# GQA attention, forward and backward, on one core: K, V, dK and dV laid out with 8 KB per partition, q and grad_out packed, every DMA on the sync queue

## The chip, the core and the metric

The kernel runs on one core of a Trainium2 chip, with nothing on the other cores. Its engines are TensorE (PE, with its weight loads shown as PEld), VectorE (DVE), ScalarE (ACT), GpSimd (POOL) and SyncE (SP); they run side by side and meet through semaphores. Data moves between DRAM and the on-chip memory by 16 DMA engines, which are fed by queues: SP's queue is called q1 in the profile, POOL's queue q0, and q8 and q14 fetch instructions. The metric is the device time of one execution in microseconds, the median over several runs.

## The reference

For 32 batches, 32 query heads with 4 query rows each share 4 key/value heads of 2,048 rows and width 128. The kernel must return the attention output and the gradients of q, k and v for a given grad_out. All tensors are bf16.

```python
B, Hq, Hkv, Sq, Sk, D = 32, 32, 4, 4, 2048, 128
k = jnp.repeat(k, rep, axis=1)
v = jnp.repeat(v, rep, axis=1)
scores = jnp.einsum("bhqd,bhkd->bhqk", q, k) * D ** -0.5
p = softmax(scores, axis=-1)
out = jnp.einsum("bhqk,bhkd->bhqd", p, v)
dq, dk, dv = vjp(grad_out)
```

K and V are read once (2 MiB each for one batch), dK and dV are written once (2 MiB each), and q, grad_out, out and dq are 32 KiB each for one batch. So a batch moves 8 MiB of large tensors and 128 KiB of small ones.

## The kernel before

One batch is cut into named units (function `units_of`, from line 172 on): loads `LQ` (q and grad_out), `LK` and `LV` (each in two pairs of heads g=0,1, 1 MiB a pair); transposes of K and V on PE (`KT`, `VT`, L372) with their copies out of PSUM (`KTe`, `VTe`, L337 on ACT or L340 on DVE); scores, maximum, exponential and row sum (`S` L383, `MX` L390, `EX` L399, `L` L402 and L404); GpSimd's scaled copies of grad_out and q (`dop` L411, `qp` L419, `rs` L423); the output (`O` L442, `Oe` L449 or L451) and its store `Os`; the gradient path (`DL` L456, `DP` L383, `DS` L463); `DV` and `DK` (L477) with their copies `DVe`, `DKe` (L483) and stores `DVs`, `DKs` (L492); and `DQ` (L442), `DQe` and the store `DQs`. ET and DT (L431) are the transposes of e and ds. For the last batch alone the stores of dV and dK go out in halves (`DVh`, `DKh`, L488).

The order is written out by hand. `plan` gives each unit a planned time, b * PERIOD plus the value of `PLACE`, plus a shift for the first three and the last four batches (`SHIFT`); all units of all batches are sorted by that time, and each engine runs its own units in that order. An engine that waits holds up all that is behind it on the same engine. That goes for SP too: a store that waits for its data holds up the loads that are planned after it. `DMA, SMALL = "SP", "POOL"` sends the large transfers to SP's queue and the small ones (`LQ`, `Os`, `DQs`) to POOL's, where they stand in line with `dop`, `qp` and `rs`.

On SP, every DMA takes the next of eight semaphores in turn, and in the built program each DMA from the ninth on waits for the DMA eight before it: no more than eight of SP's DMAs are under way at a time.

K has 8 tile buffers of 1 MiB, V has 4, and the outgoing dV and dK share 6 (`CAP`). In DRAM each head of K is 2,048 rows of 256 bytes, one after the other. A partition holds 16 rows, that is 4,096 contiguous bytes, for each of the pair's two heads; the heads are 512 KiB apart. A 1 MiB transfer is therefore 256 pieces of 4,096 bytes. q and grad_out are loaded as 128 rows of 256 bytes each, into tiles of their own for each batch, and out and dq are stored likewise.

Of the kernel before, what the change touches and what calls it, by code (L numbers as in the profile page):

```python
# [10 lines left out]
BF16 = mybir.dt.bfloat16  # L11
ACT = mybir.ActivationFunctionType
ALU = mybir.AluOpType
AX = mybir.AxisListType

P = 128
NH = 4
# [3 lines left out]
DMA, SMALL = "SP", "POOL"  # L21
# [4 lines left out]
    LQ=[-47.936], LK=[-16.977, -14.467], LV=[3.599, 0.95], QT=[-7.484], QTe=[-6.947], KT=[2.869, 1.617, 7.32, 1.994,  # L26
    -5.235, 5.431, 1.272, 6.997], KTe=[4.732, 3.093, 7.43, 5.007, -4.213, 5.728, 1.38, 7.728], VT=[10.378, 12.043,
    11.732, 10.779, 22.772, 19.387, 22.024, 28.632], VTe=[11.121, 12.155, 12.993, 11.722, 23.303, 21.604, 22.619,
    29.88], S=[7.995, 8.089, 10.109, 10.191], MX=[9.431, 10.828], EX=[11.829, 13.307], L=[13.33], dop=[14.332],
    qp=[18.579], rs=[18.682], ET=[13.658, 17.08], ETe=[14.252, 17.097], DT=[33.736, 36.072], DTe=[35.413, 37.066],  # L30
    O=[17.693, 18.002, 18.156, 18.29], Oe=[18.672], Os=[94.455], DQ=[49.509, 49.546, 51.434, 51.658], DQe=[52.911],
    DQs=[136.569], DL=[19.54], qfree=[23.411], ofree=[103.245], rfree=[77.997], DP=[19.952, 20.297, 32.139, 32.573],
# [14 lines left out]
        qp=[-26.573], rs=[12.305], ET=[-63.892, -40.448], ETe=[-47.865, -38.526], DT=[-4.086, -0.412], DTe=[-3.298,  # L47
        6.139], O=[-39.845, -33.444, -32.183, -28.165], Oe=[-27.877], Os=[-59.712], DQ=[1.765, 2.888, 1.329, 1.269],
        DQe=[1.892], DQs=[-81.021], DL=[-24.403], qfree=[-3.591], ofree=[-33.901], rfree=[9.398], DP=[-14.103,
# [6 lines left out]
        LQ=[-243.022], LK=[-211.953, -145.031], LV=[-16.995, -65.672], QT=[-143.905], QTe=[-60.636], KT=[-16.483,  # L56
        -14.108, -10.124, 0.716, -51.009, -13.779, -3.931, -2.747], KTe=[-17.567, -13.982, -6.982, -0.41, -31.758,
        -9.805, 5.197, -0.622], VT=[-0.807, 8.201, 5.214, 2.135, 10.997, 1.446, 6.104, 4.85], VTe=[0.517, 9.075,
        5.788, 2.568, 12.326, 2.03, 6.271, 3.992], S=[-0.29, 0.211, -1.108, -0.674], MX=[-1.051, -0.497], EX=[2.148,
        0.721], L=[7.117], dop=[8.675], qp=[10.349], rs=[25.4], ET=[1.855, 2.426], ETe=[1.513, 3.358], DT=[13.036,  # L60
        7.483], DTe=[12.538, 6.893], O=[3.459, 3.832, 3.884, 5.102], Oe=[4.915], Os=[-60.332], DQ=[0.889, 1.045,
        -0.411, 0.94], DQe=[0.233], DQs=[-25.356], DL=[5.409], qfree=[12.194], ofree=[-66.5], rfree=[13.969],
        DP=[6.763, 7.072, 3.675, 3.981], DS=[7.015, 3.749], DV=[6.331, 5.5, 3.952, 3.37], DVe=[5.694, 4.344, 4.713,
        4.559, 2.372, 4.222, 1.681, 2.935], DVs=[2.104, -0.302], DVh=[148.344, 585.76, 528.125, 504.253], DK=[1.08,
        3.543, 0.508, 3.091], DKe=[3.833, 4.036, 2.313, 3.472, 1.048, -0.802, 2.792, 1.943], DKs=[9.575, 1.2],
# [8 lines left out]
        O=[1.246, 1.5, 1.545, 1.726], Oe=[1.403], Os=[-52.917], DQ=[1.425, 1.546, 0.484, 0.395], DQe=[-0.47],  # L74
        DQs=[-55.959], DL=[0.669], qfree=[3.492], ofree=[-33.606], rfree=[5.069], DP=[1.794, 1.829, 0.034, -0.258],
# [10 lines left out]
        O=[-1.322, -1.479, 0.528, 1.287], Oe=[1.058], Os=[87.413], DQ=[8.174, 8.908, 7.1, 7.978], DQe=[8.064],  # L86
        DQs=[153.09], DL=[1.413], qfree=[433.476], ofree=[379.582], rfree=[188.9], DP=[2.141, 2.215, 0.855, 0.51],
# [10 lines left out]
        DTe=[13.249, 14.741], O=[4.22, 3.956, 3.979, 4.659], Oe=[5.161], Os=[124.411], DQ=[53.76, 58.627, 71.647,  # L98
        76.742], DQe=[81.838], DQs=[178.343], DL=[4.74], qfree=[223.784], ofree=[169.959], rfree=[350.347],
# [11 lines left out]
        123.716], O=[14.871, 15.992, 19.77, 20.459], Oe=[24.605], Os=[65.93], DQ=[226.498, 229.962, 296.861,  # L111
        321.979], DQe=[324.799], DQs=[716.368], DL=[24.893], qfree=[188.487], ofree=[315.264], rfree=[471.673],
# [12 lines left out]
        Oe=[158.875], Os=[319.648], DQ=[364.485, 371.073, 501.046, 588.268], DQe=[601.801], DQs=[743.423],  # L125
        DL=[177.07], qfree=[296.09], ofree=[481.606], rfree=[573.081], DP=[203.332, 207.071, 280.92, 280.696],
# [36 lines left out]
    "0131321056372566642742270600202020220020440", "5454547463637160146371372260420466424246204"]  # L163
class Unit:
# [87 lines left out]
def plan(n_batches):  # L252
    tail = {n_batches + b: b for b in SHIFT if b < 0}
    order, bank_of = [], {}
    for b in range(n_batches):
        seen, banks = collections.Counter(), iter(BANK[b])
        special = tail.get(b, b)
        for u in units_of(b):
            name = u.key[1]
            i = seen[name]  # L260
            seen[name] += 1
            u.at = b * PERIOD + PLACE[name][i] + (SHIFT[special][name][i] if special in SHIFT else 0.0)
            if len(u.eng) == 2:
                u.on = ENGINE[name][i]
                if special in SWAP and SWAP[special].get(name, "-" * 16)[i] == "x":
                    u.on = "D" if u.on == "A" else "A"
                u.on = "ACT" if u.on == "A" else "DVE"
            else:
                u.on = next(iter(u.eng), "")
            if name in (NOT_LAST if b == n_batches - 1 else ONLY_LAST):  # L270
                u.on = ""
            for r in u.opens:
                if r[1] == "ps":
                    bank_of[r] = int(next(banks))
            order.append(u)
    return sorted(order, key=lambda u: u.at), bank_of

@with_exitstack
def kernel(
    ctx: ExitStack,  # L280
    tc: tile.TileContext,
    q: bass.AP,
    k: bass.AP,
    v: bass.AP,
    grad_out: bass.AP,
# [5 lines left out]
    nc = tc.nc  # L291
    B, Hq, Sq, D = q.shape
    Hkv, Sk = k.shape[1], k.shape[2]
    assert D == P and Hq * Sq == P and Hkv == NH and Hq // Hkv * Sq == 32
# [20 lines left out]
    rows = lambda t: t.rearrange("b h s d -> b (h s) d")  # L315
    pairs = lambda t: t.rearrange("b (g h) (p c) d -> b g p h (c d)", c=C, h=2)
    q_r, go_r, o_r, dq_r = rows(q), rows(grad_out), rows(out_0), rows(out_1)
    k_r, v_r, dk_r, dv_r = pairs(k), pairs(v), pairs(out_2), pairs(out_3)
# [23 lines left out]
    def emit(u):  # L342
        b, name, arg = u.key[0], u.key[1], u.key[2:]
        t = T[b]
        if name == "LQ":
            t["q"] = sm_pool.tile([P, D], BF16, name="q_sb")
            nc.gpsimd.dma_start(out=t["q"][:], in_=q_r[b])
            t["go"] = sm_pool.tile([P, D], BF16, name="go_sb")
            nc.gpsimd.dma_start(out=t["go"][:], in_=go_r[b])
        elif name in ("LK", "LV"):  # L350
            g, = arg
            p_, src = (k_pool, k_r) if name == "LK" else (v_pool, v_r)
            x = p_.tile([P, 2, C, D], BF16, name="k_sb" if name == "LK" else "v_sb")
            for h in range(2):
                t[name[1], 2 * g + h] = x[:, h]
            whole = x[:].rearrange("p h c d -> p h (c d)")
            for h in range(2) if b == 0 else [slice(0, 2)]:
                nc.sync.dma_start(out=whole[:, h], in_=src[b, g][:, h])
        elif name == "QT":
            ps = t["qtp"] = bank(b, "qt", dt=BF16)  # L360
            nc.tensor.transpose(out=ps[:, 0, :], in_=t["q"][:], identity=ident[:])
            nc.tensor.transpose(out=ps[:, 1, :], in_=t["go"][:], identity=ident[:])
# [81 lines left out]
        elif name in ("Oe", "DQe"):  # L444
            x, by = ("o", "rinv") if name == "Oe" else ("dq", "rs")
            t[x] = sm_pool.tile([P, D], BF16, name=x + "_sb")
            src = t[name[:-1]][:, 0:D]
            if u.on == "ACT":
                nc.scalar.activation(out=t[x][:], in_=src, func=ACT.Copy, scale=t[by][:])  # L449
            else:  # L450
                nc.vector.tensor_scalar(out=t[x][:], in0=src, scalar1=t[by][:], scalar2=None, op0=ALU.mult)  # L451
        elif name in ("Os", "DQs"):
            nc.gpsimd.dma_start(out=(o_r if name == "Os" else dq_r)[b], in_=t["o" if name == "Os" else "dq"][:])
        elif name == "DL":
            t["dl"] = sm_pool.tile([P, 1], FP32, name="delta")
            nc.vector.tensor_tensor_reduce(out=junk[:], in0=t["o"][:], in1=t["go"][:], scale=1.0, scalar=0.0,  # L456
# [43 lines left out]
_INS = ['q', 'k', 'v', 'grad_out']  # L500
_OUTS = [((32, 32, 4, 128), 'bfloat16'), ((32, 32, 4, 128), 'bfloat16'), ((32, 4, 2048, 128), 'bfloat16'), ((32, 4, 2048, 128), 'bfloat16')]
# [24 lines left out]
```

## Time and profile before

| | value |
|---|---|
| median of 6 runs | 692.4 us (691.51 to 698.01) |
| the profiled execution | 698.01 us, its span 696.2 us, 1.8 us lie around the span |
| PE busy | 622.3 us, 89% |
| ACT busy | 603.5 us, 87% |
| DVE busy | 558.5 us, 80% |
| POOL busy | 207.9 us, 30% |
| DMA | 274.47 MB in 75,005 packets, mean 394 GB/s |
| read / written in DRAM | 136.31 MB / 136.31 MB |
| POOL's DMAs | 128 of 32 KB: 5.7 us (loads) and 5.9 to 6.0 us (stores) from issue to landing |
| TensorE clock granted | 0.995 of full speed |

The profiled execution is the longest of the six, 5.6 us above the median. A packet is one piece of a transfer as a DMA engine handles it; each DMA also ends in a packet of 4 bytes on each of its 16 engines that counts the semaphore up. The share of a queue is the time that its packets took, as a share of the time of all 16 engines. The shares of the four queues add up to a little over 100%, because the time in which packets of two queues are under way on one engine counts for both. DMA is near saturation in 38 of the page's 40 slices, at 380 to 417 GB/s; the first slice has 346 GB/s, the last two 257 and 262.

### The profile page before, as it was taken

Reading aid. Unit: us, or ns where it says so; the run is one execution under the profiler, and the core shown is the slowest. Engines: PE = TensorE matmul, PEld = TensorE weight load, DVE = VectorE, ACT = ScalarE, POOL = GpSimd, SP = SyncE. Lnnn points to the kernel's source line nnn. Section 1 sums busy time; section 2 is a strip of 40 time slices with the busy share of each in tenths; the row PEclk is TensorE's granted clock in tenths of the full one; section 3 lists DMA queues with packets and bytes.
Section 4 is the critical chain, followed back from the end, with each engine's and each line's share of the span. In section 5 each row is a group of like instructions: output and inputs, shape, how many; then the busy total and the mean of one; then the engine's idle time right before and its main releaser. Section 6 shows DMA issues by size and latency. Waiting matters only on the chain.

```text
span 696.2 us, 28403 instructions
## 1 busy us (share of the span) xinstructions
PE 622.3 (89%) x12352; PEld 468.6 (67%) x12352; DVE 558.5 (80%) x776; ACT 603.5 (87%) x921; POOL 207.9 (30%) x426
## 2 busy tenths in 40 slices
PE   5899999999999999989999898998898988989984
PEld 4676677777667777666767666676666766766663
DVE  2788888888888888878888878787787877878785
ACT  2889999999999999988889888899888988988883
POOL 2423321333332233331233321333312333113330
PEclk9999999999999999999999999999999999999999
DMA  8999999999999999999999999999999999999967
GB/s 346 395 393 381 417 413 412 416 415 415 416 415 410 413 399 404 397 411 411 405 408 409 406 397 408 388 393 400 402 404 398 397 387 383 408 401 389 387 257 262
DMA packets 75005, 274.47 MB, mean 394 GB/s; under 512 B 6272, under 2 KB 6272, under 8 KB 74880
## 3 DMA queue, kind: packets, MB, share of 16 engines
q1 hardware_dynamic: 70784, 268.45, 97.4%
q0 software_dynamic: 4096, 4.20, 1.8%
q8 instruction: 96, 1.57, 0.8%
q14 instruction: 29, 0.24, 0.1%
HBM read 136.31 MB, written 136.31 MB: 392 GB/s over the span
## 4 chain that ended last, share of the span: by engine, by line
DMA 53%; PE 24%; ACT 11%; issue 5%; POOL 3%; DVE 3%; SPq 0%; POOLq 0%; DVEq 0%; ACTq 0%
DMA v_sb<-in_v_dram 52%; PE psum L372 11%; PE psum L477 6%; ACT dk_sb L483 4%; ACT dv_sb L483 3%; PE psum L431 3%; PE psum L442 2%; POOL dop_sb L411 2%; ACT e_sb L399 2%; ACT vt_sb L337 1%; PE psum L383 1%; DVE kt_sb L390 1%; DMA go_sb<-in_grad_out_dram 1%; DMA out_dram<-dv_sb 1%; DVE vt_sb L340 1%
## 5 line engine op out<-in xcount | busy, mean ns | idle before, releaser
L411 POOL TENSOR_SCALAR dop_sb<-go_sb,rinv 32x128 bf16<-32x128 bf16 x128 | 76.8, 600 | 446.3 <-DVE rinv L404 272.3
L483 ACT CAST dk_sb<-psum 128x1024 bf16<-128x1024 f32 x159 | 157.6, 1013 | 26.9 <-PE psum L477 21.0
L372 PE MATMUL psum<-ident,v_sb 128*128 128x128 bf16 x2048 | 148.3, 220 | 22.1 <-DMA v_sb<-in_v_dram 20.4
L483 ACT CAST dv_sb<-psum 128x1024 bf16<-128x1024 f32 x155 | 151.7, 1023 | 13.2 <-PE psum L477 12.4
L372 PEld LDWEIGHTS <-v_sb 128*128 128x128 bf16 x2048 | 118.5, 98 | 62.8 <-issue 31.9
L372 PE MATMUL psum<-ident,k_sb 128*128 128x128 bf16 x2048 | 142.8, 221 | 10.3 <-ACT dk_sb L483 10.2
L372 PEld LDWEIGHTS <-k_sb 128*128 128x128 bf16 x2048 | 121.8, 99 | 27.2 <-issue 24.4
L483 DVE CAST dv_sb<-psum 128x1024 bf16<-128x1024 f32 x101 | 122.8, 1220 | 10.9 <-PE psum L477 10.6
L483 DVE CAST dk_sb<-psum 128x1024 bf16<-128x1024 f32 x97 | 115.9, 1219 | 8.5 <-ACT kt_sb L337 4.5
L337 ACT COPY kt_sb<-psum 128x512 f32<-128x512 f32 x190 | 110.4, 595 | 6.6 <-PE psum L372 5.4
L463 DVE SCALAR_TENSOR_TENSOR ds_sb<-psum,delta,e_sb 128x1024 bf16<-128x1024 f32 x64 | 81.9, 1279 | 21.4 <-ACT vt_sb L337 19.5
L477 PE MATMUL psum<-dop_sb,e_sb 64*128 64x256 bf16 x1024 | 90.4, 270 | 7.1 <-POOL dop_sb L411 2.0
L337 ACT COPY vt_sb<-psum 128x512 f32<-128x512 f32 x131 | 75.6, 599 | 22.7 <-PE psum L372 21.7
L340 DVE COPY vt_sb<-psum 128x1024 bf16<-128x1024 bf16 x125 | 82.9, 681 | 3.9 <-PE psum L372 3.5
L477 PE MATMUL psum<-qp_sb,ds_sb 64*128 64x256 bf16 x1024 | 81.0, 271 | 2.0 <-DVE ds_sb L463 0.8
L477 PEld LDWEIGHTS <-e_sb 64*128 64x128 bf16 x1024 | 50.0, 93 | 36.4 <-issue 19.8
L399 ACT ACTIVATE e_sb<-psum,m 128x1024 bf16<-128x1024 f32 x64 | 71.1, 1122 | 2.4 <-DVE kt_sb L390 2.2
L340 DVE COPY kt_sb<-psum 128x1024 bf16<-128x1024 bf16 x66 | 45.0, 685 | 19.7 <-PE psum L372 19.7
L477 PEld LDWEIGHTS <-ds_sb 64*128 64x128 bf16 x1024 | 43.5, 94 | 23.4 <-issue 8.9
L419 POOL TENSOR_SCALAR qp_sb<-q_sb,rinv 32x128 bf16<-32x128 bf16 x128 | 50.0, 391 | 10.3
L390 DVE TENSOR_SCALAR_CACHE_REDUCE kt_sb<-psum 128x1024 bf16<-128x1024 f32 x32 | 39.2, 1224 | 10.2 <-issue 8.1
L431 PE MATMUL psum<-ident,ds_sb 128*128 128x128 bf16 x512 | 38.9, 220 | 7.8 <-ACT e_sb L399 7.8
(46 smaller groups left out, 636.0 us busy)
## 6 DMA issues: line engine op xcount, KB each, us to landing
k_sb<-in_k_dram SPq DMA_DIRECT2D x62, 1024.0 KB, 18.8
v_sb<-in_v_dram SPq DMA_DIRECT2D x62, 1024.0 KB, 19.8
out_dram<-dv_sb SPq DMA_DIRECT2D x62, 1024.0 KB, 19.2
out_dram<-dk_sb SPq DMA_DIRECT2D x62, 1024.0 KB, 18.9
k_sb<-in_k_dram SPq DMA_DIRECT2D x4, 512.0 KB, 5.5
v_sb<-in_v_dram SPq DMA_DIRECT2D x4, 512.0 KB, 9.7
out_dram<-dv_sb SPq DMA_DIRECT2D x4, 512.0 KB, 7.9
out_dram<-dk_sb SPq DMA_DIRECT2D x4, 512.0 KB, 6.7
```

Of the source, the lines that this page charges most:

```text
L337: nc.scalar.copy(out=out.rearrange("p c d -> p (c d)").bitcast(FP32), in_=in_.rearrange("p c d -> p (c d)").bitcast(FP32))
L340: nc.vector.tensor_copy(out=out, in_=in_)
L372: nc.tensor.transpose(out=ps[:, j, :], in_=t[x, h][:, 8 * i + j, :], identity=ident[:])
L390: nc.vector.tensor_scalar(out=spent, in0=t["S", i][:], scalar1=-scale, scalar2=t["m"][:] if i else None, op0=ALU.mult, op1=ALU.min, accum_ ...
L399: nc.scalar.activation(out=t["e"][:, 2 * QW * i:2 * QW * i + 2 * QW], in_=t["S", i][:], func=ACT.Exp, bias=t["m"][:], scale=scale, accum_o ...
L411: nc.gpsimd.tensor_scalar(out=t["dop"][r, h % 2, :], in0=t["go"][r, :], scalar1=t["rinv"][r, :], scalar2=None, op0=ALU.mult)
L419: nc.gpsimd.tensor_scalar(out=t["qp"][r, h % 2, :], in0=t["q"][r, :], scalar1=t["rinv"][r, :], scalar2=scale, op0=ALU.mult, op1=ALU.mult)
L431: nc.tensor.transpose(out=ps[:, j, :], in_=src[:, P * c:P * c + P], identity=ident[:])
L442: nc.tensor.matmul(t[name][r, 0:D], lhsT=t[xt, c // 8][:, c % 8, r], rhs=t[x, h][:, c, :], start=(c == 0), stop=(c == C - 1), tile_positio ...
L463: nc.vector.scalar_tensor_tensor(out=t["ds"][:, w], in0=t["DP", i][:], scalar=t["dl"][:], in1=t["e"][:, w], op0=ALU.subtract, op1=ALU.mult)
L477: nc.tensor.matmul(accs[g][:, 2 * P * j:2 * P * j + 2 * P], lhsT=t[lhs][r, P * c:P * c + P], rhs=t[rhs][r, :, :].rearrange("p h d -> p (h ...
L483: copy(out=t[name[:2], "out", g][:, :, CPQ * i:CPQ * i + CPQ, :], in_=t[name[:2], i][g][:].rearrange("p (c h d) -> p h c d", h=2, d=D))
```

## The change

Outside the kernel, on the host, K and V are laid out anew as [batch, pair, partition, head of the pair, 16 rows * 128], so that a partition's two pieces of 4,096 bytes lie side by side: 8,192 contiguous bytes. dK and dV are written in the same layout and put back on the host. q and grad_out are packed into one tensor `qg` [partition, batch, 2, 128]; out and dq are [partition, batch, 128].

In the kernel:

- A pair's load or store is 128 pieces of 8,192 bytes. The first batch's loads still go head by head, 4,096 bytes a piece, and the last batch's dV and dK halves still have pieces of 2,048 bytes.
- `LQ` is one DMA for a group of four batches (the first group is split into batch 0 and batches 1 to 3), 9 DMAs in all. `Os` and `DQs` are one store for a group of four, after its last batch (the last group is split into batches 28 to 30 and batch 31), 9 DMAs each.
- These 27 DMAs are on SP's queue. POOL issues none. The dynamic DMA scratch buffer is cut to 1,024.
- The planned time of `Os` goes from 94.455 to 40.0 and that of `DQs` from 136.569 to 75.0, and their shifts for the first and last batches become those of `Oe` and `DQe`. No other planned time, engine choice or PSUM bank changes.
- The tiles `qg_sb`, `o_sb` and `dq_sb` hold a group each, with two buffers.

```diff
-DMA, SMALL = "SP", "POOL"
+DMA, SMALL = "SP", "SP"
+GROUP = 4
...
-... Os=[94.455] ... DQs=[136.569]
+... Os=[40.0] ... DQs=[75.0]
...
+def group_of(b, n_batches, name):
+    first = b - b % GROUP
+    last = min(first + GROUP, n_batches) - 1
+    if name == "LQ":
+        cuts = [first, first + 1, last + 1] if first == 0 else [first, last + 1]
+    else:
+        cuts = [first, last, last + 1] if last == n_batches - 1 else [first, last + 1]
+    lo = max(c for c in cuts if c <= b)
+    return lo, min(c for c in cuts if c > b)
...
+            if name in ("LQ", "Os", "DQs"):
+                lo, hi = group_of(b, n_batches, name)
+                if b != (lo if name == "LQ" else hi - 1):
+                    u.on = ""
...
-            t["q"] = sm_pool.tile([P, D], BF16, name="q_sb")
-            nc.gpsimd.dma_start(out=t["q"][:], in_=q_r[b])
-            t["go"] = sm_pool.tile([P, D], BF16, name="go_sb")
-            nc.gpsimd.dma_start(out=t["go"][:], in_=go_r[b])
+            lo, hi = group_of(b, B, name)
+            x = sm_pool.tile([P, GROUP, 2, D], BF16, name="qg_sb", bufs=2)
+            nc.sync.dma_start(out=x[:, :hi - lo], in_=qg[:, lo:hi])
+            for j in range(lo, hi):
+                T[j]["q"], T[j]["go"] = x[:, j - lo, 0], x[:, j - lo, 1]
...
-            x = p_.tile([P, 2, C, D], BF16, name="k_sb" if name == "LK" else "v_sb")
+            x = p_.tile([P, 2, C * D], BF16, name="k_sb" if name == "LK" else "v_sb")
             for h in range(2):
-                t[name[1], 2 * g + h] = x[:, h]
-            whole = x[:].rearrange("p h c d -> p h (c d)")
+                t[name[1], 2 * g + h] = x[:, h].rearrange("p (c d) -> p c d", d=D)
             for h in range(2) if b == 0 else [slice(0, 2)]:
-                nc.sync.dma_start(out=whole[:, h], in_=src[b, g][:, h])
+                nc.sync.dma_start(out=x[:, h], in_=src[b, g][:, h])
...
-            t[x] = sm_pool.tile([P, D], BF16, name=x + "_sb")
+            lo, hi = group_of(b, B, x)
+            if b == lo:
+                T[lo][x + "s"] = sm_pool.tile([P, GROUP, D], BF16, name=x + "_sb", bufs=2)
+            t[x] = T[lo][x + "s"][:, b - lo]
...
-            nc.gpsimd.dma_start(out=(o_r if name == "Os" else dq_r)[b], in_=t["o" if name == "Os" else "dq"][:])
+            x, dst = ("o", o_r) if name == "Os" else ("dq", dq_r)
+            lo, hi = group_of(b, B, x)
+            nc.sync.dma_start(out=dst[:, lo:hi], in_=T[lo][x + "s"][:, :hi - lo])
...
-_OUTS = [((32, 32, 4, 128), 'bfloat16'), ((32, 32, 4, 128), 'bfloat16'), ((32, 4, 2048, 128), 'bfloat16'), ((32, 4, 2048, 128), 'bfloat16')]
+_OUTS = [(128, 32, 128), (128, 32, 128), (32, 2, 128, 2, 2048), (32, 2, 128, 2, 2048)]
...
+    rows = lambda x: x.reshape(B, P, D).transpose(1, 0, 2)
+    pairs = lambda x: x.reshape(B, 2, 2, P, S // P, D).transpose(0, 1, 3, 2, 4, 5).reshape(B, 2, P, 2, S // P * D)
+    sent = dict(qg=_np.stack([rows(q), rows(go)], axis=2), k=pairs(k), v=pairs(v))
+    nc = _bacc.Bacc("TRN2", target_bir_lowering=False, num_devices=1, dynamic_dma_scratch_size=1024)
```

More of the change, by code (lines that the diff above doesn't have):

```diff
@@ L30 @@
     qp=[18.579], rs=[18.682], ET=[13.658, 17.08], ETe=[14.252, 17.097], DT=[33.736, 36.072], DTe=[35.413, 37.066],
-    O=[17.693, 18.002, 18.156, 18.29], Oe=[18.672], Os=[94.455], DQ=[49.509, 49.546, 51.434, 51.658], DQe=[52.911],
-    DQs=[136.569], DL=[19.54], qfree=[23.411], ofree=[103.245], rfree=[77.997], DP=[19.952, 20.297, 32.139, 32.573],
+    O=[17.693, 18.002, 18.156, 18.29], Oe=[18.672], Os=[40.0], DQ=[49.509, 49.546, 51.434, 51.658], DQe=[52.911],
+    DQs=[75.0], DL=[19.54], qfree=[23.411], ofree=[103.245], rfree=[77.997], DP=[19.952, 20.297, 32.139, 32.573],
     DS=[20.684, 33.191], DV=[17.102, 19.055, 20.709, 23.293], DVe=[18.269, 19.578, 20.009, 20.012, 22.48, 21.535,
@@ L47 @@
         qp=[-26.573], rs=[12.305], ET=[-63.892, -40.448], ETe=[-47.865, -38.526], DT=[-4.086, -0.412], DTe=[-3.298,
-        6.139], O=[-39.845, -33.444, -32.183, -28.165], Oe=[-27.877], Os=[-59.712], DQ=[1.765, 2.888, 1.329, 1.269],
-        DQe=[1.892], DQs=[-81.021], DL=[-24.403], qfree=[-3.591], ofree=[-33.901], rfree=[9.398], DP=[-14.103,
+        6.139], O=[-39.845, -33.444, -32.183, -28.165], Oe=[-27.877], Os=[-27.877], DQ=[1.765, 2.888, 1.329, 1.269],
+        DQe=[1.892], DQs=[1.892], DL=[-24.403], qfree=[-3.591], ofree=[-33.901], rfree=[9.398], DP=[-14.103,
         -13.278, -0.13, 0.179], DS=[-3.43, 2.07], DV=[-22.144, -22.96, -21.745, -14.349], DVe=[-21.142, -24.454,
@@ L60 @@
         0.721], L=[7.117], dop=[8.675], qp=[10.349], rs=[25.4], ET=[1.855, 2.426], ETe=[1.513, 3.358], DT=[13.036,
-        7.483], DTe=[12.538, 6.893], O=[3.459, 3.832, 3.884, 5.102], Oe=[4.915], Os=[-60.332], DQ=[0.889, 1.045,
-        -0.411, 0.94], DQe=[0.233], DQs=[-25.356], DL=[5.409], qfree=[12.194], ofree=[-66.5], rfree=[13.969],
+        7.483], DTe=[12.538, 6.893], O=[3.459, 3.832, 3.884, 5.102], Oe=[4.915], Os=[4.915], DQ=[0.889, 1.045,
+        -0.411, 0.94], DQe=[0.233], DQs=[0.233], DL=[5.409], qfree=[12.194], ofree=[-66.5], rfree=[13.969],
         DP=[6.763, 7.072, 3.675, 3.981], DS=[7.015, 3.749], DV=[6.331, 5.5, 3.952, 3.37], DVe=[5.694, 4.344, 4.713,
@@ L73 @@
         qp=[5.002], rs=[10.293], ET=[1.766, 0.607], ETe=[1.259, 1.305], DT=[0.213, -2.004], DTe=[-0.525, -2.044],
-        O=[1.246, 1.5, 1.545, 1.726], Oe=[1.403], Os=[-52.917], DQ=[1.425, 1.546, 0.484, 0.395], DQe=[-0.47],
-        DQs=[-55.959], DL=[0.669], qfree=[3.492], ofree=[-33.606], rfree=[5.069], DP=[1.794, 1.829, 0.034, -0.258],
+        O=[1.246, 1.5, 1.545, 1.726], Oe=[1.403], Os=[1.403], DQ=[1.425, 1.546, 0.484, 0.395], DQe=[-0.47],
+        DQs=[-0.47], DL=[0.669], qfree=[3.492], ofree=[-33.606], rfree=[5.069], DP=[1.794, 1.829, 0.034, -0.258],
         DS=[2.187, -0.275], DV=[3.733, 2.494, 1.983, 0.34], DVe=[2.697, 1.941, 1.905, 2.434, 1.012, 1.581, 0.049,
@@ L85 @@
         qp=[7.309], rs=[42.149], ET=[2.195, -1.278], ETe=[1.919, -1.171], DT=[4.743, 3.278], DTe=[5.609, 3.25],
-        O=[-1.322, -1.479, 0.528, 1.287], Oe=[1.058], Os=[87.413], DQ=[8.174, 8.908, 7.1, 7.978], DQe=[8.064],
-        DQs=[153.09], DL=[1.413], qfree=[433.476], ofree=[379.582], rfree=[188.9], DP=[2.141, 2.215, 0.855, 0.51],
+        O=[-1.322, -1.479, 0.528, 1.287], Oe=[1.058], Os=[1.058], DQ=[8.174, 8.908, 7.1, 7.978], DQe=[8.064],
+        DQs=[8.064], DL=[1.413], qfree=[433.476], ofree=[379.582], rfree=[188.9], DP=[2.141, 2.215, 0.855, 0.51],
         DS=[2.76, 0.829], DV=[2.494, 0.835, 0.895, 0.758], DVe=[1.61, 0.109, 1.229, 0.024, -0.073, 2.137, -1.76,
@@ L97 @@
         dop=[6.256], qp=[8.124], rs=[52.601], ET=[1.369, 4.066], ETe=[2.632, 4.831], DT=[11.561, 14.267],
-        DTe=[13.249, 14.741], O=[4.22, 3.956, 3.979, 4.659], Oe=[5.161], Os=[124.411], DQ=[53.76, 58.627, 71.647,
-        76.742], DQe=[81.838], DQs=[178.343], DL=[4.74], qfree=[223.784], ofree=[169.959], rfree=[350.347],
+        DTe=[13.249, 14.741], O=[4.22, 3.956, 3.979, 4.659], Oe=[5.161], Os=[5.161], DQ=[53.76, 58.627, 71.647,
+        76.742], DQe=[81.838], DQs=[81.838], DL=[4.74], qfree=[223.784], ofree=[169.959], rfree=[350.347],
         DP=[4.904, 5.645, 9.011, 8.772], DS=[5.688, 11.455], DV=[4.558, 4.643, 5.415, 6.214], DVe=[4.631, 4.282,
@@ L110 @@
         qp=[19.591], rs=[195.2], ET=[16.601, 13.645], ETe=[17.156, 15.506], DT=[91.107, 112.344], DTe=[91.851,
-        123.716], O=[14.871, 15.992, 19.77, 20.459], Oe=[24.605], Os=[65.93], DQ=[226.498, 229.962, 296.861,
-        321.979], DQe=[324.799], DQs=[716.368], DL=[24.893], qfree=[188.487], ofree=[315.264], rfree=[471.673],
+        123.716], O=[14.871, 15.992, 19.77, 20.459], Oe=[24.605], Os=[24.605], DQ=[226.498, 229.962, 296.861,
+        321.979], DQe=[324.799], DQs=[324.799], DL=[24.893], qfree=[188.487], ofree=[315.264], rfree=[471.673],
         DP=[25.295, 26.106, 46.944, 48.701], DS=[28.132, 55.939], DV=[14.792, 16.553, 22.109, 26.604], DVe=[14.274,
@@ L124 @@
         128.051], DT=[266.776, 395.941], DTe=[293.717, 431.921], O=[134.296, 138.938, 140.503, 143.271],
-        Oe=[158.875], Os=[319.648], DQ=[364.485, 371.073, 501.046, 588.268], DQe=[601.801], DQs=[743.423],
+        Oe=[158.875], Os=[158.875], DQ=[364.485, 371.073, 501.046, 588.268], DQe=[601.801], DQs=[601.801],
         DL=[177.07], qfree=[296.09], ofree=[481.606], rfree=[573.081], DP=[203.332, 207.071, 280.92, 280.696],
@@ L281 @@
     tc: tile.TileContext,
-    q: bass.AP,
+    qg: bass.AP,
     k: bass.AP,
     v: bass.AP,
-    grad_out: bass.AP,
     out_0: bass.AP,
@@ L291 @@
     nc = tc.nc
-    B, Hq, Sq, D = q.shape
-    Hkv, Sk = k.shape[1], k.shape[2]
-    assert D == P and Hq * Sq == P and Hkv == NH and Hq // Hkv * Sq == 32
+    B, D = qg.shape[1], qg.shape[3]
+    Sk = k.shape[4] // D * P
+    assert D == P and qg.shape[0] == P
     C = Sk // P
@@ L313 @@
     make_identity(nc, ident[:])
[L315 to L318, printed above, removed]
+    o_r, dq_r = out_0, out_1
+    k_r, v_r, dk_r, dv_r = k, v, out_2, out_3
     order, bank_of = plan(B)
@@ L352, in emit @@
             p_, src = (k_pool, k_r) if name == "LK" else (v_pool, v_r)
-            x = p_.tile([P, 2, C, D], BF16, name="k_sb" if name == "LK" else "v_sb")
+            x = p_.tile([P, 2, C * D], BF16, name="k_sb" if name == "LK" else "v_sb")
             for h in range(2):
-                t[name[1], 2 * g + h] = x[:, h]
-            whole = x[:].rearrange("p h c d -> p h (c d)")
+                t[name[1], 2 * g + h] = x[:, h].rearrange("p (c d) -> p c d", d=D)
             for h in range(2) if b == 0 else [slice(0, 2)]:
-                nc.sync.dma_start(out=whole[:, h], in_=src[b, g][:, h])
+                nc.sync.dma_start(out=x[:, h], in_=src[b, g][:, h])
         elif name == "QT":
             ps = t["qtp"] = bank(b, "qt", dt=BF16)
-            nc.tensor.transpose(out=ps[:, 0, :], in_=t["q"][:], identity=ident[:])
-            nc.tensor.transpose(out=ps[:, 1, :], in_=t["go"][:], identity=ident[:])
+            nc.tensor.transpose(out=ps[:, 0, :], in_=t["q"], identity=ident[:])
+            nc.tensor.transpose(out=ps[:, 1, :], in_=t["go"], identity=ident[:])
         elif name == "QTe":
@@ L445, in emit @@
             x, by = ("o", "rinv") if name == "Oe" else ("dq", "rs")
-            t[x] = sm_pool.tile([P, D], BF16, name=x + "_sb")
+            lo, hi = group_of(b, B, x)
+            if b == lo:
+                T[lo][x + "s"] = sm_pool.tile([P, GROUP, D], BF16, name=x + "_sb", bufs=2)
+            t[x] = T[lo][x + "s"][:, b - lo]
             src = t[name[:-1]][:, 0:D]
             if u.on == "ACT":
-                nc.scalar.activation(out=t[x][:], in_=src, func=ACT.Copy, scale=t[by][:])
+                nc.scalar.activation(out=t[x], in_=src, func=ACT.Copy, scale=t[by][:])
             else:
-                nc.vector.tensor_scalar(out=t[x][:], in0=src, scalar1=t[by][:], scalar2=None, op0=ALU.mult)
+                nc.vector.tensor_scalar(out=t[x], in0=src, scalar1=t[by][:], scalar2=None, op0=ALU.mult)
         elif name in ("Os", "DQs"):
-            nc.gpsimd.dma_start(out=(o_r if name == "Os" else dq_r)[b], in_=t["o" if name == "Os" else "dq"][:])
+            x, dst = ("o", o_r) if name == "Os" else ("dq", dq_r)
+            lo, hi = group_of(b, B, x)
+            nc.sync.dma_start(out=dst[:, lo:hi], in_=T[lo][x + "s"][:, :hi - lo])
         elif name == "DL":
             t["dl"] = sm_pool.tile([P, 1], FP32, name="delta")
-            nc.vector.tensor_tensor_reduce(out=junk[:], in0=t["o"][:], in1=t["go"][:], scale=1.0, scalar=0.0,
+            nc.vector.tensor_tensor_reduce(out=junk[:], in0=t["o"], in1=t["go"], scale=1.0, scalar=0.0,
                                            op0=ALU.mult, op1=ALU.add, accum_out=t["dl"][:])
@@ L498 @@
                 emit(u)
-_INS = ['q', 'k', 'v', 'grad_out']
-_OUTS = [((32, 32, 4, 128), 'bfloat16'), ((32, 32, 4, 128), 'bfloat16'), ((32, 4, 2048, 128), 'bfloat16'), ((32, 4, 2048, 128), 'bfloat16')]
+_OUTS = [(128, 32, 128), (128, 32, 128), (32, 2, 128, 2, 2048), (32, 2, 128, 2, 2048)]
 def kernel(**inputs):
@@ L508 @@
     from concourse.bass_utils import run_bass_kernel_spmd as _run
-    nc = _bacc.Bacc("TRN2", target_bir_lowering=False, num_devices=1)
+    q, k, v, go = (_np.asarray(inputs[x]) for x in ("q", "k", "v", "grad_out"))
+    B, H, S, D = k.shape
+    rows = lambda x: x.reshape(B, P, D).transpose(1, 0, 2)
+    pairs = lambda x: x.reshape(B, 2, 2, P, S // P, D).transpose(0, 1, 3, 2, 4, 5).reshape(B, 2, P, 2, S // P * D)
+    sent = dict(qg=_np.stack([rows(q), rows(go)], axis=2), k=pairs(k), v=pairs(v))
+    nc = _bacc.Bacc("TRN2", target_bir_lowering=False, num_devices=1, dynamic_dma_scratch_size=1024)
     arrays, args = {}, []
-    for name in _INS:
-        a = _np.ascontiguousarray(inputs[name])
-        if a.dtype.kind in "iu":
-            a = a.astype(_np.int64)
+    for name, a in sent.items():
+        a = _np.ascontiguousarray(a)
         arrays[f"in_{name}_dram"] = a
         args.append(nc.dram_tensor(f"in_{name}_dram", a.shape, _mybir.dt.from_np(a.dtype), kind="ExternalInput").ap())
-    for i, (shape, dtype) in enumerate(_OUTS):
-        dt = _mybir.dt.from_np(_np.dtype(dtype))
-        args.append(nc.dram_tensor(f"out_{i}_dram", shape, dt, kind="ExternalOutput").ap())
+    for i, shape in enumerate(_OUTS):
+        args.append(nc.dram_tensor(f"out_{i}_dram", shape, BF16, kind="ExternalOutput").ap())
     with _tile.TileContext(nc) as tc:
@@ L523 @@
     r = _run(nc, [arrays], core_ids=[0])
-    got = tuple(r.results[0][f"out_{i}_dram"] for i in range(len(_OUTS)))
-    return got
+    o, dq, dk, dv = (r.results[0][f"out_{i}_dram"] for i in range(len(_OUTS)))
+    unrows = lambda x: x.transpose(1, 0, 2).reshape(q.shape)
+    unpairs = lambda x: x.reshape(B, 2, P, 2, S // P, D).transpose(0, 1, 3, 2, 4, 5).reshape(k.shape)
+    return unrows(o), unrows(dq), unpairs(dk), unpairs(dv)
```

## The prediction

> **What bounds the kernel now.** I read the page first: its busy shares, its DMA queues and the chain that ended last.
>
> ```profile
> PE 622.3 (89%) x12352; PEld 468.6 (67%) x12352; DVE 558.5 (80%) x776; ACT 603.5 (87%) x921; POOL 207.9 (30%) x426
> ...
> q1 hardware_dynamic: 70784, 268.45, 97.4%
> q0 software_dynamic: 4096, 4.20, 1.8%
> ...
> DMA 53%; PE 24%; ACT 11%; issue 5%; POOL 3%; DVE 3%; SPq 0%; POOLq 0%; DVEq 0%; ACTq 0%
> ...
> v_sb<-in_v_dram SPq DMA_DIRECT2D x62, 1024.0 KB, 19.8
> ```
>
> SP's queue fills 97.4% of the DMA engines' time, and the V loads make half of the chain, but PE and ACT are close behind. A load lands 19.8 us after its issue although 1 MiB needs only 2.6 us at 400 GB/s, so seven or eight transfers stand in line: DMA engines, not SP's issuing, set that delay. Next the chain in order of time (start, length, what), which says where each bound rules:
>
> ```profile
> 87.01 1.89 PE psum L372 x32
> ...
> 249.65 1.89 PE psum L372 x32
> ...
> 279.77 21.81 DMA v_sb<-in_v_dram
> 301.64 21.11 DMA v_sb<-in_v_dram
> ```
> ```profile
> 634.88 1.89 PE psum L372 x32
> ```
>
> The same PE mark recurs once a batch. From 87.01 to 249.65 are 8 batches, 20.33 us each, and the chain there is PE, ACT and DVE: this is the compute pace. To 634.88 are 18 batches, 21.40 us each, and each is one V load: an issue that waits for the eighth DMA before it, in other words DMA pace. The windows view over these stretches (length, busy time of the engines, clock, DMA share, GB/s), and the DMA view of the first and second of them:
>
> ```profile
> 87.01:249.65 162.64, 153.79 (x3089) 116.42 (x3090) 138.32 (x194) 151.43 (x232) 49.64 (x101) 1.00 1.03 413
> 249.65:634.88 385.23, 348.03 (x6950) 261.95 (x6950) 311.77 (x434) 340.98 (x521) 114.38 (x232) 1.00 1.02 401
> ```
> ```profile
> q1 hardware_dynamic: 17065, 65.79, 100.0%
> q0 software_dynamic: 869, 0.89, 1.6%
> ```
> ```profile
> q1 hardware_dynamic: 39195, 151.12, 99.4%
> q0 software_dynamic: 2212, 2.27, 1.7%
> ```
>
> DMA is full in both. In the first, q1 moved 65.79 MB, 7.84 batches of 8.389 MB, so DMA needed 20.74 us a batch where compute took 20.33; a lead of early loads covered the gap and was spent by 250 us. In the second DMA needed 385.23/18.01 = 21.39 us.
>
> **The large transfers.** q1's time per packet: in the first stretch 162.64 us x 16 engines x 100.0% = 2,602 us, less some 1,000 semaphore packets (4 bytes, 9 ns), over 65.79 MB / 4,096 B = 16,062 packets gives 161 ns; packet by packet, the trace's median for 4,096 bytes is 159 ns. At the end of the run the packets have 2,048 bytes (stores in halves): from 688 to 692 us the view has 669 packets, 1.27 MB, 84.9%, which is 54 us for 620 data packets, 87 ns (median packet 84). Doubling the bytes from 2,048 to 4,096 adds 75 ns, so a packet costs 9 ns plus 36.6 ns per 1,000 bytes. No q1 packet has 8,192 bytes, but instruction queue q14 has; this is one, alone in a window of 1 us from 456 us:
>
> ```profile
> q14 instruction: 1, 0.01, 1.9%
> ```
>
> 1.9% of 16 us is 304 ns; the median over the trace's 35 is 309, just what 9 + 300 gives. So two packets of 4,096 (318 ns) become one of 309. The change makes 31,744 such packets (64,512 of 4,096 before, less 1,024 that the first batch keeps, halved): 31,744 x 9 ns / 16 = 17.9 us less, 0.58 us a batch. The ends: no packet overhead at all would be 300 ns, 35.7 us less. The other end is q8, whose 16 KB packets took 0.8% of 696.2 x 16 us / 96 = 928 ns, 464 for 8 KB: 31,744 x 146 / 16 = 290 us more. I take 309, since it is the same size in the same loaded engines; q8's packets alternate with q1's, and 928 less two of q1's 159 is 610, close to 9 + 600.
>
> The Trainium skill (DMA: Bandwidth & Descriptors, "SWDGE vs HWDGE vs iDMA") speaks against this: a packet, the unit at which an engine switches queues, has preferably at most 4,096 bytes. If SP's queue cut its pieces there, this term would be 0 instead of -17.9; this trace has packets of 8 and 16 KB, though on instruction queues alone.
>
> **The small transfers.** Removed: 128 DMAs of POOL, 1.8% x 696.2 = 12.5 us of all engines. Added on q1: 1,152 packets of 512 to 2,048 bytes and 2,304 of 256 to 1,024, by 9 ns + 36.6 ns/1,000 B about 185 us of packets with 27 x 16 semaphores, /16 = 11.6 us. Equal, if nothing ran for free before. But the shares of the second stretch add to 102.1%: if q0 had really run beside q1, moving it would cost up to its 1.7%, 11.8 us. Against that, q1's packets there average 166 ns instead of 159 (385.23 x 16 x 99.4% / 36,895 = 166), and this stretching is what waiting for another queue's packet looks like. I take +1, range -1 to +11.
>
> **Start and end.** PE's first work waited for POOL's small loads, the grad_out load from 2.32 us for 6.28; K transposes began at 8.73 and had all of K. Now SP issues this load first, one issue (some 0.45 us) ahead of K; PE can start near 4 us and is then paced by K: the quickest of its first four pieces of 512 KB landed 3.9 us after its issue, so here near 5, the other three 1.3 us apart, the last near 9, and its transposes take 1.5 us more: 10.6 where they ended at 14.7. Compute may gain 4 us; DMA, full from the start, at most 1 or 2. I take -1. At the end:
>
> ```profile
> 684.48 3.70 SPq L488 DMA_DIRECT2D out_dram<-dk_sb  x4
> ...
> 689.08 0.35 DVE L451 TENSOR_SCALAR dq_sb<-psum,rs 128x128 bf16<-128x128 f32 x1 [1.52 <-issue]
> 689.73 0.54 POOL L453 DMA_DIRECT2D out_dram<-dq_sb  x1 [4.18 <-DVE dq_sb L451]
> ```
>
> The last dq store ended the run, 6.3 us after its issue. In the changed program's order it stands on SP ahead of the four dK halves, which so cannot leave at 684.48 but after 689.4: five issues of 0.4 us, and 2 MB at 400 GB/s takes 5.2 us, landing near 697 instead of 696.2. +1, at most +3.
>
> **Waits moved to SP.** The 18 grouped stores wait for `Oe` or `DQe`, planned 21 or 22 us earlier, and behind them stand V and K loads, which PE needs. The cover is the seven transfers in line, some 18 us of DMA work; without it each us of waiting costs one. The grouped loads wait for POOL's `qp` two groups back, two batches earlier. Both 0. POOL loses 4 issues of 0.55 us a batch; it is 30% busy and idles before `dop` waiting for DVE's 1/l: 0.
>
> **The sum.** -17.9 + 1 - 1 + 1 = -16.9: on the profiled execution 698.0 - 16.9 = 681, on the median 692.4 - 16.9 = 675.5; the packet count is the same in both. The second bound is compute: were all 18 slow batches run at 20.33, the span would lose 18 x 1.07 = 19.3 and be 676.9, 678.7 with the 1.8 outside it; with 4 us gained at the start 675. Both bounds now stand at 675 to 679, and where two meet neither hides the other's hiccups. I forecast **677 us**.
>
> **Rivals.** (a) SP's queue cuts pieces at 4,096 bytes, so the change does not do what it says. For: q1 has nothing above 4,096 today; against: today no piece is longer. Time: 692.4 + 1 - 1 + 1 = 693, 689 if the small loads' gain at the start counts in full. Chance 0.12. (b) The small transfers were free and now stand in q1's line: 692.4 - 17.9 + 11 - 1 + 1 = 685.5. For: 102.1%; against: stretched packets. 0.12. (c) Slower: packets of 8,192 bytes, read or written at twice the pitch by 16 engines at once, take longer than two of 4,096. Its price is 31,744 packets / 16 = 1.98 us for each ns above 318; from 320 ns on the kernel is slower by 0.5%, at 330 it takes 692.4 + 24 + 1 = 717. For: q8's row; against: q14's. 0.08. The forecast keeps 0.68, with 670 to 683 its own range.
>
> **How the numbers follow.** About 0.5%, 3.5 us, is what a measurement can tell from no change; faster means below 688.9. That takes the forecast, (b), and a small part of (a): 0.82. Same: most of (a), 0.09. Slower: (c) and the far part of (a), 0.09. The range runs from 668 to 689. Its lower end: in the first stretch PE is busy 153.79 of 162.64 us, so with a DMA that is never short the compute pace could fall from 20.33 to 19.2 at the least; a quarter of that over 26 batches is 7 us, 675 - 7 = 668, and the 300 ns end is cut off by the same bound. The upper end takes in (b) and leaves out most of (a) and all of (c), together some 0.2.
>
> **What would show it.** Right: q1 has about 42,900 packets (31,744 + 1,024 + 2,048 + 3,456 + 291 x 16), no q0, and its time per 8 KB is near 320 ns with stalls; the chain has PE and ACT where V loads stood, a batch near 20.5 us. (a) would show some 74,700 packets, (b) batches of 21 us with PE waiting for V, (c) a lower GB/s at full share. At the end the dK halves would land last. Wrong it would be if DMA's pace fell but compute waited for something new, say a load behind a store on SP.

## The result: a shade slower, and the profile after

The changed kernel takes 696.04 us (median of 21 runs, 694.02 to 697.4) where the kernel before takes 692.67 (47 runs, 690.37 to 698.01): a ratio of 1.0045, 95% interval 1.0035 to 1.0056. Forecast were 677 us, 668 to 689. The profiled execution took 696.77 us, its span is 695.0. Its page, in the same lines as before (busy shares; DMA queues with packets, MB and share; the chain by engine):

```profile
PE 622.0 (90%) x12352; PEld 469.4 (68%) x12352; DVE 559.0 (80%) x776; ACT 603.4 (87%) x921; POOL 132.0 (19%) x298
...
q1 hardware_dynamic: 42928, 272.65, 96.4%
...
DMA 35%; PE 34%; ACT 20%; issue 4%; DVE 2%; POOL 1%; SPq 1%; ACTq 0%; DVEq 0%; POOLq 0%
```

The packets are the 42,900 that were forecast, POOL's queue is gone, and the chain has lost a third of its DMA share to PE and ACT. So the large packets are whole, and DMA rules less of the run. The chain in order of time shows that the change also works in the middle:

```profile
331.17 1.89 PE psum L385 x32
351.41 1.89 PE psum L385 x32
...
383.69 18.35 DMA v_sb<-in_v_dram
402.10 21.04 DMA v_sb<-in_v_dram
...
584.39 2.40 PE psum L385 x40
```

The batches keep the compute pace until 351 us (most marks are 20.24 us apart; the 13 batches from the mark at 87.24 us on take 20.32 on average), where the kernel before left it at 250 us. The PE piece of 40 transposes at 584.39 us is the one that the chain before has at 592.45:

```profile
592.45 2.40 PE psum L372 x40
```

By there 8 us are won against the profiled execution before, less against a typical one, since that execution is 5.3 us above its median. In the rest of the run 7 us are lost again: from this mark to the end of the span are 103.8 us before and 110.6 after. The timeline of SP's issues at the end (start, time until the last issue, operation, count):

```profile
648.17 0.34 SPq L471 DMA_DIRECT2D out_dram<-o_sb  x1
648.61 0.87 SPq L510 DMA_DIRECT2D out_dram<-dk_sb  x2
651.71 1.63 SPq L510 DMA_DIRECT2D out_dram<-dv_sb  x2
667.00 0.33 SPq L471 DMA_DIRECT2D out_dram<-o_sb  x1
675.55 0.33 SPq L471 DMA_DIRECT2D out_dram<-dq_sb  x1
675.94 1.01 SPq L510 DMA_DIRECT2D out_dram<-dk_sb  x2
676.99 5.29 SPq L506 DMA_DIRECT2D out_dram<-dv_sb  x4
682.38 1.34 SPq L471 DMA_DIRECT2D out_dram<-dq_sb  x1
683.77 5.60 SPq L506 DMA_DIRECT2D out_dram<-dk_sb  x4
```

Counted from the end, the large stores are dK of batch 29 (648.61), dV of 30, dK of 30 (675.94), and the halves of dV and dK of batch 31. SP stands at a small store three times, as the waits view says (line, who was waited for, total, times, longest; L471 is the out or dq store):

```profile
SPq L471 <- DVE delta L474: 23.0, 2, 13.9
...
SPq L471 <- ACT dq_sb L465: 8.1, 1, 8.1
```

The two waits of the first line are those of the out store of batches 28 to 30, 9.1 us until 648.17, and of batch 31, 13.9 us until 667.00; the second line is the dq store of batches 28 to 30. Finished data lies behind them: dK of batch 29, complete at 643.47 us, leaves at 648.61, and dK of batch 30 (2 MiB), complete at 663.72, leaves only at 675.94, with dV of batch 31 behind it. The last dq copy is 9.2 us earlier than before (689.08):

```profile
679.89 0.35 DVE L467 TENSOR_SCALAR dq_sb<-psum,rs 128x128 bf16<-128x128 f32 x1 [1.52 <-issue]
```

But at 675.94 us there were still 6 MiB to be written. The last 50 us of the DMA view in 40 slices, busy tenths and mean GB/s of the changed kernel and then the busy tenths of the kernel before:

```profile
DMA  3017999999961100002000000799989999999950
GB/s 138 20 39 297 419 413 419 419 413 411 406 243 46 39 26 26 20 20 51 2 0 0 0 0 13 288 419 413 413 356 380 387 387 378 361 390 387 382 198 0
```
```profile
DMA  9999999999953999920101999999999999992000
```

DMA stands all but still for 16 us (13 slices of 1.25 us in the middle) and then writes until some 2 us before the end; before, the gap was 6 us.

### The profile page after: what moved, and what is told of

It is laid out like the page before. It is cut to its first block, busy times and chain, and to the rows that moved or that the text cites. A ratio compares the mean times of both kernels' runs of the same rounds, so it can differ in the third digit from the quotient of the medians.

```text
span 695.0 us, 28243 instructions
## 1 busy us (share of the span) xinstructions
PE 622.0 (90%) x12352; PEld 469.4 (68%) x12352; DVE 559.0 (80%) x776; ACT 603.4 (87%) x921; POOL 132.0 (19%) x298
## 4 chain that ended last, share of the span: by engine, by line
DMA 35%; PE 34%; ACT 20%; issue 4%; DVE 2%; POOL 1%; SPq 1%; ACTq 0%; DVEq 0%; POOLq 0%
DMA v_sb<-in_v_dram 30%; PE psum L385 16%; PE psum L495 9%; ACT dk_sb L501 8%; ACT dv_sb L501 5%; PE psum L444 4%; ACT e_sb L412 3%; DMA out_dram<-dk_sb 3%; PE psum L455 3%; ACT vt_sb L350 2%; PE psum L396 2%; DMA qg_sb<-in_qg_dram 2%; ACT et_sb L350 1%; POOL dop_sb L424 1%; DVE kt_sb L403 1%
## 5 line engine op out<-in xcount | busy, mean ns | idle before, releaser
L424 POOL TENSOR_SCALAR dop_sb<-qg_sb,rinv 32x128 bf16<-32x128 bf16 x128 | 76.4, 597 | 521.2 <-DVE rinv L417 229.3
L432 POOL TENSOR_SCALAR qp_sb<-qg_sb,rinv 32x128 bf16<-32x128 bf16 x128 | 46.9, 366 | 10.5
L403 DVE TENSOR_SCALAR_CACHE_REDUCE kt_sb<-psum,m 128x1024 bf16<-128x1024 f32 x32 | 41.1, 1284 | 6.6 <-DVE kt_sb L403 3.6
```

What stands on the lines that cost most here:

```text
L403: nc.vector.tensor_scalar(out=spent, in0=t["S", i][:], scalar1=-scale, scalar2=t["m"][:] if i else None, op0=ALU.mult, op1=ALU.min, accum_ ...
L424: nc.gpsimd.tensor_scalar(out=t["dop"][r, h % 2, :], in0=t["go"][r, :], scalar1=t["rinv"][r, :], scalar2=None, op0=ALU.mult)
L432: nc.gpsimd.tensor_scalar(out=t["qp"][r, h % 2, :], in0=t["q"][r, :], scalar1=t["rinv"][r, :], scalar2=scale, op0=ALU.mult, op1=ALU.mult)
```

## The experiments

Ratios are to the kernel before on the same chip, with their 95% interval.

**The end alone.** Four planned times of the changed kernel are moved, so that no small store stands in front of a finished large one:

```diff
 -2: dict(
-    Os=[24.605] ... DQs=[324.799]
+    Os=[171.0] ... DQs=[618.0]
 -1: dict(
-    Os=[158.875] ... DQs=[601.801]
+    Os=[418.7] ... DQs=[709.7]
```

> The changed kernel with only the planned times of the last small stores moved: out of batches 28 to 30 goes behind dV of batch 30, out of batch 31 behind dK of batch 30, dq of 28 to 30 behind the dV halves of batch 31, dq of 31 behind its dK halves. Theory T (at the end SP stands at the grouped dq and out stores while 6 MB of finished dK and dV wait behind them): the last dq copy stays near 680 us in the profile, the end comes some 6 to 8 us after it instead of 15, and the time falls by 7 to 11 us, to 685 to 689. Rival R (the end is late because compute and the loads before it are late; the stores only wait in another order): under 2 us, 694 or more.

Measured: 687.81 us, 0.992 (0.9903 to 0.9938); 8.2 us less than the changed kernel. SP's issues at its end and the last 50 us of its DMA:

```profile
662.03 0.81 SPq L510 DMA_DIRECT2D out_dram<-dk_sb  x2
665.53 0.33 SPq L471 DMA_DIRECT2D out_dram<-o_sb  x1
666.66 4.95 SPq L506 DMA_DIRECT2D out_dram<-dv_sb  x4
674.09 0.34 SPq L471 DMA_DIRECT2D out_dram<-dq_sb  x1
674.48 3.70 SPq L506 DMA_DIRECT2D out_dram<-dk_sb  x4
678.80 0.73 SPq L471 DMA_DIRECT2D out_dram<-dq_sb  x1
```
```profile
DMA  9999998999613999920101999999798359999000
```

dK of batch 30 leaves 13.9 us earlier, though the last dq copy (678.42) is only 1.5 us earlier, and the span ends 7.0 us after that copy instead of 15.1. DMA's gap is back at 6 us. Theory T holds, rival R falls.

**The layout alone.** The kernel before, with this only (and the loads, host and output lines that go with it):

```diff
-    k_r, v_r, dk_r, dv_r = pairs(k), pairs(v), pairs(out_2), pairs(out_3)
+    k_r, v_r, dk_r, dv_r = k, v, out_2, out_3
```

> The kernel before with the 8,192-byte layout alone; q, grad_out, out and dq stay on POOL's queue in single batches. Theory T: the end is as before, the middle gains what the change gained (8 us at 584 us against the profiled run, some 3 to 8 against a typical one), so 683 to 688. Rival R: the middle's gain is lost by waits for compute whatever the end does, 690 or more. Rival Q (small transfers were cheaper on POOL's queue, beside q1): below 683, as the packets alone would give 675.

Measured: 687.38 us, 0.9915 (0.9898 to 0.9932): 6 us won, a third of the 17.9 forecast. Its chain in order of time:

```profile
352.89 1.89 PE psum L370 x32
373.14 1.89 PE psum L370 x32
380.38 21.04 DMA v_sb<-in_v_dram
```

PE's marks stand in the chain until 373 us, some 120 us longer than before the change, though not all at 20.25 us: from 85.68 us on they are 20.53 apart on average. Then each batch is one V load and DMA sets a pace near 21, not the 20.2 to 20.8 that 0.58 us a batch would give. Theory T holds; rivals R and Q fall.

**The queue alone.** The changed kernel with K, V, dK and dV head by head in DRAM, 4,096 bytes a piece:

```diff
-    k_r, v_r, dk_r, dv_r = k, v, out_2, out_3
+    pairs = lambda t: t.rearrange("b g h p c -> b g p h c")
+    k_r, v_r, dk_r, dv_r = pairs(k), pairs(v), pairs(out_2), pairs(out_3)
```

> The changed kernel with K, V, dK and dV head by head in DRAM again, pieces of 4,096 bytes; small transfers packed and on SP's queue as changed. Theory T: no gain in the middle and the loss at the end, 692.7 + 7 to 11, so 700 to 704, with DMA idle for over 10 us near the end as in the changed kernel. Rival R: within 3 us of 693. Rival Q: 704 or more, with the middle slower than before by 0.2 to 0.4 us a batch.

Measured: 701.18 us, 1.0107 (1.0086 to 1.0128). The loss is there without the layout, and of the same size as what the late small stores gave back (8.5 and 8.2 us). DMA stands all but still for 17 us near the end. Theory T holds.

**The queue alone, with the late small stores.** Both of the edits above:

> The small transfers packed and on SP's queue, with the late planned times at the end, and pieces of 4,096 bytes as before the change: the fourth corner beside the kernel before, the layout alone and the two together. Theory T (the blocked end is all that the queue move costs): 701.2 - 8 = 693, equal to the kernel before within 1.5 us. Rival Q (small transfers in q1's line cost in the middle): 696 or more.

Measured: 691.41 us, 0.9995 (0.9977 to 1.0012): equal to the kernel before. With this the four corners are filled:

| ratio to the kernel before | small stores as changed | small stores late | small ones on POOL, as before |
|---|---|---|---|
| 4,096 bytes a piece | 1.0107 | 0.9995 | 1 |
| 8,192 bytes a piece | 1.0045 | 0.9920 | 0.9915 |

Down each column the layout gives 0.6 to 0.9%, along each row the order at the end costs 1.1 to 1.3%, and the last two columns agree within 0.05%: the small transfers cost nothing on SP's queue that these intervals, some 0.2% wide to each side, would show, as long as nothing finished stands behind them.

**Compute's own pace.** The kernel with the late small stores, and the dV stores of batches 4 to 27 left out:

```diff
+            if name == "DVs" and 4 <= b < 28:
+                u.on = ""
```

> As the first of these, with the dV stores of batches 4 to 27 left out (48 MiB less to write; dV of these batches stays unwritten): DMA has 2.6 us less to do for each of their two stores, so the middle runs at the pace of compute alone. If compute's pace is 20.25 us a batch, the mark at 584 us moves to 573 and the time to some 675. If compute can go faster with DMA out of its way, a batch is under 20 us and the time under 670. If waits other than DMA hold the middle, it stays at 20.7 or more, 683 or more.

Measured: 677.61 us (one execution). The windows view from 100 to 560 us, of this kernel and then of the one with all stores (length, busy time of PE, PEld, DVE, ACT, POOL, clock, DMA share, GB/s):

```profile
100.00:560.00 460.00, 432.69 (x8676) 327.76 (x8673) 388.04 (x539) 427.07 (x653) 93.74 (x207) 1.00 0.85 319
```
```profile
100.00:560.00 460.00, 430.68 (x8640) 325.38 (x8640) 385.52 (x537) 425.03 (x648) 92.85 (x207) 1.00 1.01 416
```

With DMA at 85% PE waits for no transfer in this window. The maxima of successive batches start 20.2 to 20.5 us apart for most of the run, at times up to 21.4, and never below 20.2 in the middle. So with this order compute alone takes some 678 us, and 10 us are left above it in the best version.

**DMA by itself.** Three kernels copy K to dK and V to dV, 1 MiB a transfer, with eight of SP's DMAs under way; attention is left out. They differ in the pieces alone: 8,192, 4,096 and 2,048 bytes.

```diff
+    LAG = 4
...
+        for n in range(len(work) + LAG):
+            if n < len(work):
...
+                nc.sync.dma_start(out=tiles[n][:], in_=src[b, g])
+            if n >= LAG:
...
+                nc.sync.dma_start(out=dst[b, g], in_=tiles.pop(n - LAG)[:])
```

> DMA alone: K is copied to dK and V to dV through the same tiles, 1 MiB a transfer, 8,192 bytes a piece, all on SP's queue with 8 under way; no attention is computed and the small outputs stay unwritten. 32,768 packets of 309 ns on 16 engines are 633 us, with semaphores 635; with the start and the last landing some 640. If packets in this mix of reads and writes stall as in the kernel (319 ns), 655 to 660.

> The same copy with K, V, dK and dV head by head in DRAM, 4,096 bytes a piece. 65,536 packets of 159 ns are 651 us, with the rest some 658. Theory P (a packet costs 9 ns): 18 us more than the copy with 8,192 bytes. Rival (the longer piece gains little because something else sets DMA's pace): under 9 us more.

> The copy alone with pieces of 2,048 bytes; attention is left out and the small outputs stay unwritten, as in the other copies. From the steady 500 us of those, an engine takes 155.1 ns for each packet of 4,096 bytes and 305.6 for 8,192 (time divided by packets), so a packet costs 4.6 ns and 2,048 bytes 75.3: 131,072 packets of 79.9 ns are 654 us, with semaphores and ends 666. If the recorded 84 ns were what an engine spends, 688 and with the ends 699.

Measured: 637.37, 646.02 and 665.69 us (two executions each). The second takes 8.65 us more than the first, not the 18 of theory P; that was the rival's range. The DMA view of 500 us in the middle (packets, MB, share of 16 engines), in the same order:

```profile
q1 hardware_dynamic: 29338, 213.65, 101.1%
```
```profile
q1 hardware_dynamic: 54592, 210.46, 102.5%
```
```profile
q1 hardware_dynamic: 102853, 204.27, 105.1%
```

One queue alone, and its share is above 100%, the more so the smaller the packets: the recorded durations of successive packets overlap. 16 x 500 us divided by the packets gives what an engine spends: 305.6 ns for 8,192 bytes and 155.1 for 4,096 (26,080 and 51,382 packets, a share of the semaphore packets taken off), where the records say 309 and 159. A packet costs 4.6 ns, half of 9. The third copy was forecast from that, 666 us, and took 665.7; with the recorded 84 ns it would have been 699. So the rival's reason, another thing that sets DMA's pace, is not needed: a price by packet and by byte fits all three copies.

**Two ideas on one long batch.** In the changed kernel the maximum of batch 28 starts 24.7 us after that of batch 27 (25.4 with the late small stores), in the layout alone 21.6. V comes late there (waits of the window 564 to 594 us):

```profile
PE psum L385 <- DMA v_sb<-in_v_dram: 2.9, 1, 2.9
```

Ahead of these V loads (550.70 us), with only two dV stores between, SP issues the dq store of batches 20 to 23 and the q load of batches 28 to 31 (540.58 and 543.36 us), two small DMAs among the eight under way. The first kernel has the late small stores and this load a batch earlier (`LQ=[16.855]` becomes `LQ=[-1.4]` for batch 28); the second has the late small stores and sends all 27 packed transfers from POOL (`nc.gpsimd.dma_start`).

> The kernel with the late small stores, and one planned time more: the q and grad_out load of batches 28 to 31 goes one batch earlier, so that it no longer stands right behind the dq store of batches 20 to 23 on SP. Theory S (of SP's eight DMAs under way two were small ones there, the V loads of batch 28 came 2.9 us late and that batch took 25 us instead of 21): the long batch falls to 21 to 22.5 and the time by 2 to 4 us against its parent, to 684 to 686. Rival (the batch is long because DMA is behind there, whatever stands in line): the long batch stays or only moves, and the time is within 1.5 us of 687.8.

> The kernel with the late small stores, but the 27 packed transfers on POOL's queue instead of SP's; the 8,192-byte layout stays. Theory S: no small DMA takes one of SP's eight places, the long batch near 570 us is gone: 683 to 686. Rival Q (small transfers in q1's line cost their full time in the middle, 0.36 us a batch over the 13 DMA-bound batches): 4 to 5 us less than 687.8, every DMA-bound batch shorter by 0.3 to 0.4. Neither: 687 to 690, because POOL's queue now has packets that stretch q1's, or its waits hold up dop.

Measured: 687.19 us, 0.992 (0.9907 to 0.9933), and 688.02 us, 0.9927 (0.9914 to 0.9941). In both the long batch shrinks, to 22.5 and 22.2 us, but the time does not follow: the kernel that they start from has 0.992. So the times that theory S gave were missed twice, and rival Q falls here too. Nor does the shrinking speak for theory S alone. In the changed kernel's profile TensorE's granted clock falls to half just after PE's wait for V, as the windows view shows (length, busy time of PE, PEld, DVE, ACT, POOL, then the clock):

```profile
571.70:575.00 3.30, 3.30 (x33) 2.27 (x30) 0.90 (x1) 2.55 (x5) 0.00 (x0) 0.50 1.02 432
```

With the late small stores it is half for some 6.8 us there; in the two kernels of this experiment and in the layout alone it is full from 560 to 600 us. In the first of the two V still comes 2.0 us late. So part of the shrinking is the clock and part V's earlier landing; no run separates them, nor shows what lowers the clock.

## Why the prediction was wrong

The forecast was -16.9 us and +3.4 came. Two terms of the sum failed: the layout's was three times too large, and the end's was put at 1 us where it is 8.

**The bounds** were read rightly. Compute's pace of 20.33 us was given a bound of 675 to 679 us; with DMA eased it is 677.6.

**"31,744 x 9 ns / 16 = 17.9 us less"** was mis-sized twice. The 9 ns came from recorded durations (84 and 159, with 309 beside them), which overlap; in time divided by packets it is 4.6 ns, and the copies differ by 8.65 us. The shares of q1 alone near 100% in the stretches before, beside 1.6 to 1.8% of q0, were the hint; the text took the surplus over 100% for the work of two queues, but the copies pass 100% with one. And the term was taken over all 32 batches, though DMA set the pace in 18 of them by the text's own reading; in the others a faster DMA only builds a lead. 6 us of the 8.65 show; that the lead explains the rest is argued, not tested. The end of the range, 300 ns and no overhead, was not wrong as a bound. Rival (a) falls: q1's 31,744 packets of 8,192 bytes are whole.

**"Both bounds now stand at 675 to 679"** followed from that: without the loss at the end the time is 687 or so, well above compute.

**The small transfers, "+1, range -1 to +11"**: 0 by the columns of the table, to within some 1 us. Rival (b) falls.

**"I take -1" for the start**: 0. The first piece of K let PE begin at 6.00 us, but the last wait for K ended at 10.88, not 9, and the transposes at 15.33; the mark at 87.01 us before stands at 87.24.

**"+1, at most +3" for the end** is the step that failed outright: it is 8 us. The text followed the last dq store and the four dK halves behind it, but not the same thing earlier: out of batches 28 to 30 ahead of dK of batch 29, and out of batch 31 and dq of batches 28 to 30 ahead of dK of batch 30 and dV of batch 31. "Waits moved to SP" priced the grouped stores at nothing, with two covers, the planned distance of 21 or 22 us and the seven transfers in line. Neither holds at the end. The planned distance is still there, but the shifts of the last batches stretch planned time: dq of batch 30 is copied at 1,016.7 in the plan and stored at 1,038.8, dK of batch 30 follows at 1,091.1, and no other transfer of SP stands between the copy and the store. And with no loads left the line runs dry. The price was named there, a microsecond for each one without cover, but the place was not looked for, though the order of SP's instructions showed it.

Of the rivals none came true: no cut pieces, no slow packets. What happened was the sentence at the end of the prediction, with a store in place of a load: finished stores behind a waiting one on SP.

The sum with the measured terms: 692.7 - 5.9 (layout) + 0 (queue) + 8.2 (end) = 695.0, and 696.0 was measured.

What stays open: why DMA's packets stretch late in the run. In the copies 99 of 100 packets of 8,192 bytes take at most 311 ns by their records; in the changed kernel the mean record is 314 ns from 100 to 350 us and 334 from 560 to 630 us. No run here separates a cause.

## What to carry to other kernels

When waiting transfers are put on a queue that runs in order, list what stands behind each of them at the very end, where no prefetched work covers the wait; a store that is grouped over four batches waits for the last of them, and all that stands behind it waits too. Here the grouping stayed, and four planned times gave 8 us back. And take a packet's price from time divided by packets of a saturated stretch, not from the recorded duration of one packet.

## What the runs showed of the hardware

- SP's queue moves 8,192-byte pieces as single packets (31,744 of them in the changed kernel), and with reads and writes mixed 16 engines sustain 427 GB/s with them, 421 with 4,096 and 409 with 2,048 (the three copies, 100 to 600 us).
- Recorded packet durations on one queue overlap: 101.1, 102.5 and 105.1% of the engines' time. A share near 100% therefore says that a queue is saturated, not what a packet costs.
